# A fused attention and gated feed-forward kernel on one core: wide attention layout from the second unit, all of the first unit's weights in two parts, a new written order and three aligned places

## The chip, the core and the metric

The kernel runs on one core of a Trainium2 chip. The metric is the device time of one execution in microseconds (us). The kernel before took 614.35 us (median of three runs, 613.45 to 615.07).

## The reference

```python
# q, k, v: (8, 8, 576, 64); window 64, causal
scores = q @ k.T / 8, masked to 0 <= row - col < 64
attn = softmax(scores) @ v                 # per head
x = attn, heads side by side               # (8, 576, 512)
x_prev = x shifted by one row, zeros first # per batch
xk = mu_k * x + (1 - mu_k) * x_prev
xr = mu_r * x + (1 - mu_r) * x_prev
kk = relu(xk @ w_k) ** 2                   # (8, 576, 1024)
out = sigmoid(xr @ w_r) * (kk @ w_v)       # (8, 576, 512)
```

The three weight matrices are 64-bit floats in memory; all else is 32-bit.

## The kernel before, in words

**Units.** The 4608 rows (8 batches of 576) are cut into nine units of 512. A unit needs three products, computed transposed: r (`r_units`: 4 output tiles of 128, each summed over 4 chunks of 128 inputs), k (`k_units`: 8 tiles, 4 chunks) and v (`v_units`: 4 tiles, 8 chunks). That is 16 + 32 + 32 = 80 pieces of 128x128 by 128x512. I write R0, K0, V0 for the products of the first unit, R1, K1, V1 for those of the second.

**A product in two parts.** A piece is normally three fp32r matmuls: weight and input are each split into a high and a low part, and high*high, high*low and low*high are added up (`product`, `weight`). So a 512-column weight block must be decoded and split before it is used, and so must the mixed input. `DIRECT = "rk"` makes an exception: in the first unit, r and k use the unsplit weight (tile `whole`) and the unsplit input (tile `xm`) in one fp32 matmul per piece, which the compiler issues as two instructions. The weights are split later, for the second unit.

**Weights.** There are 20 blocks of 128x512 (`chunks`): 0 to 3 are w_r, 4 to 11 w_k, 12 to 19 w_v. For each, `decode` makes a 32-bit number out of the 64-bit one in five steps: sign (ACT), clamp (DVE or POOL), shift, top and low (DVE). Then come first_part (a cast, ACT or POOL) and second_part (a subtraction, POOL or DVE), which split it.

**Mixing.** `mix` makes xr and xk of one chunk: diff, blend (DVE), from the second unit on seam, and, where the product is split, high (cast) and low (subtraction).

**Attention.** A unit has four groups (a pair of heads each), so there are 36 groups and 18 pairs j = 0 to 17 of groups. The first unit (groups 0 to 3, `WHOLES = 4`) uses full 128x128 blocks and TensorE transposes. Later groups work in bands of 32 rows: `scores` multiplies in 64x32 tiles of the array; softmax runs on DVE and ACT (`soften`); DVE transposes; `values` multiplies in 32x64 tiles; `run_x` copies the result out. Below `WIDE = 8` a group's four bands each hold four blocks, so `values` takes 6 steps of 8 matmuls per group. From `WIDE` on a pair of groups shares bands: two bands of a group with eight blocks each, 5 steps of 8 matmuls per group, and one accumulation over both groups of the pair. In that layout the scores of a group need both groups' loads.

**The order.** The program is straight-line, and each engine works its instructions in order. The order is computed while the program is built: every piece of work has a key, costs in ns, needs and holds on buffers. `play` steps through time and lets each engine start the piece with the lowest key that is ready. For the first part of the program this choice is overruled by `ORDER`, a written list of piece numbers per engine: about 850 pieces, up to about 145 us. After that the keys decide, with a fixed pattern per unit. `clocked` models TensorE's time of a piece.

**Aligned places.** `values` can emit `addr_align`, which pads TensorE's instruction stream with empty slots until the next instruction stands at a given offset in a block of so many 64-byte slots; if more than `max_nops` slots are needed, the stream jumps over them. `PLACED = 18` makes this never happen in the kernel before, since j ends at 17.

Every operation is recorded through one helper, line 166, so the profile's rows are told apart by their tiles: `bank<-xm,whole` is an fp32 product, `bank<-xs,ws` a split r or k product, `bank<-ks,ws` a v product, `bank<-qk` scores, `bank<-pt,v` values, `ws<-` the split of a weight, `xs<-` that of an input, `ks<-` that of k squared.

## Time and profile before

| | |
|---|---|
| median of three runs | 614.35 us |
| the profiled execution | 613.81 us |
| its span on the core | 612.0 us |
| TensorE matmul busy | 596.7 us |
| DVE, ACT, POOL busy | 395.0, 371.0, 141.9 us |
| granted TensorE clock | 1.0 in every slice |

PE is TensorE's matmuls, PEld its weight loads, DVE the vector engine, ACT the scalar engine, POOL GpSimd, SP the engine that issues the loads and stores. Matmul ends are modelled, so the distance between two starts is a better length of a run of matmuls than its busy time.

### The profile page before, as it was taken

The numbers are of one execution on the slowest core, as the hardware profiler recorded it, in microseconds if no ns is written. First come the engines' busy times: TensorE is split into PE (matmuls) and PEld (weight loads), VectorE is DVE, ScalarE is ACT, GpSimd is POOL, SyncE is SP. The second block draws the span as 40 slices with busy tenths as digits, with TensorE's granted clock in tenths as the row PEclk, the third lists the DMA queues.
The fourth block names the chain that finished last, engine by engine and source line by source line (L and its number), as shares of the span: only waits on it lengthen the run. The fifth ranks groups of instructions, "written<-read, shape, count | busy, mean of one in ns | idle before, by whom it ended". The sixth has DMA issues, their size and how long they took to land.

```text
span 612.0 us, 17692 instructions
## 1 busy us (share of the span) xinstructions
PE 596.7 (98%) x7072; PEld 465.6 (76%) x7072; DVE 395.0 (65%) x1208; ACT 371.0 (61%) x1060; POOL 141.9 (23%) x208
## 2 busy tenths in 40 slices
PE   4999999999999999999999999999999999999997
PEld 3654577878888888888888888877888888888885
DVE  4899999909783667556763677276827583665211
ACT  5988967448476736683577358644766466734630
POOL 6575557502300230011201130023002300201000
PEclk9999999999999999999999999999999999999999
DMA  8997122213431223122312222132212230010001
GB/s 252 337 331 224 54 86 81 70 51 83 132 93 43 76 73 116 29 75 71 101 42 59 91 77 74 44 109 80 76 44 93 74 97 24 2 54 17 1 18 52
DMA packets 57426, 53.59 MB, mean 88 GB/s; under 512 B 10496, under 2 KB 50944, under 8 KB 57344
## 3 DMA queue, kind: packets, MB, share of 16 engines
q1 hardware_dynamic: 57344, 52.46, 28.1%
q8 instruction: 56, 0.92, 0.6%
q14 instruction: 26, 0.21, 0.1%
HBM read 43.00 MB, written 9.44 MB: 86 GB/s over the span
## 4 chain that ended last, share of the span: by engine, by line
PE 88%; DMA 7%; ACT 2%; DVE 1%; SPq 1%; issue 1%; ACTq 0%
PE bank L166 88%; DMA raw<-w_v 3%; DMA v<-v 2%; SPq L166 1%; DMA raw<-w_k 1%; DMA qk<-kT 1%; ACT pr L166 1%; DVE bank L166 1%; ACT kf L166 1%; DVE r L166 0%; ACT ws L166 0%; ACT wt L166 0%; DVE rs L166 0%; ACT ks L166 0%; DVE whole L166 0%
## 5 line engine op out<-in xcount | busy, mean ns | idle before, releaser
L166 PE MATMUL bank<-xs,ws 128*128 128x512 f32 x1152 | 273.2, 396 | 0.0
L166 PEld LDWEIGHTS bank<-xs,ws 128*128 128x128 f32 x1152 | 215.8, 188 | 50.9
L166 PE MATMUL bank<-ks,ws 128*128 128x512 f32 x864 | 206.7, 397 | 1.4 <-issue 1.4
L166 PEld LDWEIGHTS bank<-ks,ws 128*128 128x128 f32 x864 | 161.0, 188 | 40.2 <-issue 1.5
L166 DVE TENSOR_TENSOR ks<-kf,ks 128x512 fp32r<-128x512 f32 x69 | 51.1, 746 | 112.9 <-ACT ks L166 112.9
L166 ACT ACTIVATE pr<-pr,nmax 128x96 f32<-128x96 f32 (+1 forms) x288 | 105.0, 366 | 11.7 <-DVE nmax L166 11.1
L166 ACT ACTIVATE kf<-bank 128x512 f32<-128x512 f32 x72 | 43.0, 597 | 67.3 <-PE bank L166 65.4
L166 POOL CAST ks<-kf 128x512 fp32r<-128x512 f32 x8 | 4.9, 611 | 256.0 <-ACT kf L166 256.0
L166 DVE CUSTOM_DVE_ANT_0 pr<-bank,bands 128x96 f32<-128x96 f32 x256 | 49.4, 249 | 13.4 <-PE bank L166 13.2
L166 ACT COPY xT<-bank 128x256 f32<-128x256 f32 (+1 forms) x46 | 15.7, 391 | 65.1 <-PE bank L166 64.9
L166 ACT ACTIVATION_READ_ACCUMULATOR pr<-pr,nmax 128x1 f32 x288 | 54.1, 188 | 0.0
L166 ACT ACTIVATE kf<-kf 128x512 f32<-128x512 f32 x71 | 44.7, 631 | 1.9
L166 DVE SCALAR_TENSOR_TENSOR r<-bank,r 128x512 f32<-128x512 f32 x36 | 24.5, 680 | 32.3 <-PE bank L166 32.3
L166 PE MATMUL bank<-xm,whole 128*128 128x512 f32 x96 | 43.8, 601 | 1.0 <-DVE whole L166 1.0
L166 ACT ACTIVATE th<-bank 128x512 f32<-128x512 f32 x36 | 21.3, 591 | 35.8 <-PE bank L166 24.6
L166 PEld LDWEIGHTS bank<-pt,v 32*64 32x64 f32 (+1 forms) x2720 | 35.7, 131 | 9.4 <-issue 7.1
L166 ACT CAST ks<-kf 128x512 fp32r<-128x512 f32 x64 | 39.5, 619 | 1.7
L166 PE MATMUL bank<-qk 64*32 64x96 f32 (+1 forms) x2112 | 33.4, 254 | 7.3 <-DMA qk<-qT 5.9
L166 PEld LDWEIGHTS bank<-qk 64*32 64x32 f32 (+1 forms) x2112 | 28.2, 108 | 15.3 <-issue 12.5
L166 PE MATMUL bank<-pt,v 32*64 32x96 f32 (+3 forms) x2720 | 38.6, 243 | 0.3 <-ACT kf L166 0.3
L166 DVE TENSOR_TENSOR xs<-d,xs 128x512 fp32r<-128x512 f32 x59 | 37.9, 685 | 0.0
L166 ACT CAST xs<-d 128x512 fp32r<-128x512 f32 x49 | 28.8, 617 | 14.2 <-POOL d L166 12.7
(79 smaller groups left out, 547.4 us busy)
## 6 DMA issues: line engine op xcount, KB each, us to landing
v<-v SPq DMA_DIRECT2D x76, 64.0 KB, 2.1
raw<-w_k SPq DMA_DIRECT2D x8, 512.0 KB, 7.2
raw<-w_v SPq DMA_DIRECT2D x8, 512.0 KB, 5.6
v<-v SPq DMA_DIRECT2D x52, 48.0 KB, 2.0
v<-v SPq DMA_DIRECT2D x68, 32.0 KB, 2.0
raw<-w_r SPq DMA_DIRECT2D x4, 512.0 KB, 6.0
outT<-r SPq DMA_DIRECT2D x8, 256.0 KB, 2.1
qk<-kT SPq DMA_DIRECT2D x8, 224.0 KB, 4.2
```

The source lines that it names most:

```text
L166: return lambda *args, **kw: tc.keep_in_program_order(op(*args, **kw))
```

## The change

`DIRECT` becomes empty, so the first unit's r and k are split products like all others: three fp32r matmuls instead of two fp32 instructions per piece, and `mix` does high and low for the first unit too. `WIDE` becomes 4, so pairs 2 and 3 (the second unit) get the layout with two bands and eight blocks, and their loads are made in pairs of groups. The mask that was made for the third unit is made once for both layouts' first blocks. `play` charges TensorE for a change between tiled (attention) and untiled matmuls (`ENTER`, `LEAVE`), some costs are new, and `ORDER` is a new list. `values` aligns TensorE's stream ahead of pairs 3, 6 and 11.

In the new list TensorE does `S4` between the two transposes of group 2, then R0; scores 8 and 9 stand together (apart before), values 4 and 5 and values 8 and 9 too, and scores 10 and 11 come before most of K1.

```diff
-DIRECT = "rk"
+DIRECT = ""
-WIDE = 8
+WIDE = 4
-ALIGN, SKIP = 102, 12
-PLACED = 18
+PLACES, SKIP = {3: 228, 6: 59, 11: 59}, 12
+ENTER, LEAVE = 95, 281
 ORDER = {
...
-        moved, clock = 0, [WINDOW, 0, True]
+        moved, clock, tiled = 0, [WINDOW, 0, True], None
...
-                        free[e] = p.done = clocked(now, p.costs[e])
+                        work, at = p.costs[e], now
+                        before, tiled = tiled, work not in (440, 697, WHOLE)
+                        if before is not None and tiled != before:
+                            at = clocked(at, ENTER if tiled else LEAVE, 1)
+                        free[e] = p.done = clocked(at, work, 1.8 if tiled else 2.37 if work == 440 else 1.92)
...
-            if j >= PLACED:
-                tc.keep_in_program_order(nc.tensor.addr_align(128, offset=ALIGN, max_nops=SKIP))
+            if j in PLACES:
+                tc.keep_in_program_order(nc.tensor.addr_align(256, offset=PLACES[j], max_nops=SKIP))
...
-        if g >= NC:
-            load_qk(g, key=begin(g - 1) - 1)
-            load_v(g, key=begin(g) - 1)
+        for x in range(g, g + 2) if g >= WIDE and g % 2 == 0 else [g] if NC <= g < WIDE else []:
+            load_qk(x, key=begin(x - 1) - 1)
+            load_v(x, key=begin(x) - 1)
...
-            built = chain["masks"] = Piece("POOL", begin(g) - 4, 900, lambda e: first_mask(e, 0), [built, chain["least"]], port=True)
+            built = chain["masks"] = Piece("POOL", begin(g) - 4, 900, lambda e: first_mask(e, 0, 2), [built, chain["least"]], port=True)
...
-        if 2 * j % NC == 0 and u in (2, 4):
+        if 2 * j % NC == 0 and u == 4:
```

## Rows read from the trace of the kernel before

**Rows 1.** The page's first part: busy us, share, instructions of each engine.
```profile
PE 596.7 (98%) x7072; PEld 465.6 (76%) x7072; DVE 395.0 (65%) x1208; ACT 371.0 (61%) x1060; POOL 141.9 (23%) x208
```

**Rows 2.** Windows: stretch, length, busy of PE, PEld, DVE, ACT, POOL, clock, DMA.
```profile
15.00:30.00 15.00, 15.00 (x238) 10.06 (x232) 13.29 (x61) 13.66 (x52) 8.58 (x15) 1.00 0.94 332
30.00:45.00 15.00, 15.00 (x153) 8.17 (x148) 14.24 (x39) 13.49 (x38) 11.59 (x15) 1.00 1.02 336
45.00:60.00 15.00, 14.04 (x95) 5.99 (x94) 14.93 (x31) 14.35 (x33) 7.22 (x8) 1.00 0.77 236
60.00:78.00 18.00, 17.65 (x270) 9.14 (x272) 17.25 (x61) 15.64 (x51) 10.67 (x18) 1.00 0.23 63
78.00:98.00 20.00, 20.00 (x429) 15.97 (x415) 19.69 (x34) 13.04 (x26) 10.04 (x11) 1.00 0.20 58
98.00:118.00 20.00, 20.00 (x88) 16.16 (x87) 19.60 (x56) 12.81 (x48) 16.00 (x15) 1.00 0.39 115
...
123.00:166.50 43.50, 43.50 (x608) 35.22 (x608) 24.71 (x72) 25.40 (x70) 10.17 (x15) 1.00 0.32 90
```

**Rows 3.** Timeline of PE, later part: start, length, operation, count, idle before.
```profile
156.22 2.06 PE L166 MATMUL bank<-pt,v 32*64 32x96 f32 x160
158.21 8.63 PE L166 MATMUL bank<-ks,ws 128*128 128x512 f32 x36
...
204.29 1.73 PE L166 MATMUL bank<-qk 64*32 64x96 f32 x128
205.95 14.27 PE L166 MATMUL bank<-ks,ws 128*128 128x512 f32 x60
...
415.82 8.65 PE L166 MATMUL bank<-ks,ws 128*128 128x512 f32 x36 [1.36 <-issue]
...
552.50 33.63 PE L166 MATMUL bank<-xs,ws 128*128 128x512 f32 x144
585.97 22.45 PE L166 MATMUL bank<-ks,ws 128*128 128x512 f32 x96
```

**Rows 4.** Timeline of PE, one unbroken run of fp32 products.
```profile
35.33 10.57 PE L166 MATMUL bank<-xm,whole 128*128 128x512 f32 x24
```

**Rows 5.** Timeline of PE, 71 to 125 us.
```profile
73.86 1.65 PE L166 MATMUL bank<-ks,ws 128*128 128x512 f32 x6
75.36 1.88 PE L166 MATMUL bank<-xm,whole 128*128 128x512 f32 x4
77.16 1.31 PE L166 MATMUL bank<-pt,v 32*64 32x96 f32 x96
78.40 7.93 PE L166 MATMUL bank<-ks,ws 128*128 128x512 f32 x33
86.26 2.40 PE L166 MATMUL bank<-pt,v 32*64 32x96 f32 x192
88.59 5.14 PE L166 MATMUL bank<-ks,ws 128*128 128x512 f32 x21
93.67 1.00 PE L166 MATMUL bank<-qk 64*32 64x96 f32 x64
94.60 1.66 PE L166 MATMUL bank<-ks,ws 128*128 128x512 f32 x6
...
123.11 1.17 PE L166 MATMUL bank<-pt,v 32*64 32x96 f32 x80
124.21 0.96 PE L166 MATMUL bank<-xs,ws 128*128 128x512 f32 x3
```

**Rows 6.** Groups by form: busy us, mean ns of one, idle before.
```profile
L166 ACT ACTIVATE pr<-pr,nmax 128x96 f32<-128x96 f32 x256 | 92.6, 363 | 7.6 <-DVE nmax L166 7.1
...
L166 ACT CAST xs<-d 128x512 fp32r<-128x512 f32 x49 | 28.8, 617 | 14.2 <-POOL d L166 12.7 <-DVE d L166 0.8 <-PE bank L166 0.6
```

**Rows 7.** Timeline of DVE: second parts of blocks 13 and 19, the last mix.
```profile
72.01 0.69 DVE L166 TENSOR_TENSOR ws<-wt,ws 128x512 fp32r<-128x512 f32 x1
72.61 0.25 DVE L166 CUSTOM_DVE_ANT_0 pr<-bank,bands 128x96 f32<-128x96 f32 x1
...
96.94 0.69 DVE L166 TENSOR_TENSOR ws<-wt,ws 128x512 fp32r<-128x512 f32 x1
97.54 0.25 DVE L166 CUSTOM_DVE_ANT_0 pr<-bank,bands 128x96 f32<-128x96 f32 x1
...
116.95 0.68 DVE L166 TENSOR_TENSOR xs<-d,xs 128x512 fp32r<-128x512 f32 x1
117.55 0.42 DVE L166 TENSOR_SCALAR r<-r 128x512 f32<-128x512 f32 x1
```

**Rows 8.** Timeline of DVE at 88 us, one subtraction.
```profile
88.09 1.77 DVE L166 TENSOR_TENSOR ws<-whole,ws 128x512 fp32r<-128x512 f32 x1
```

**Rows 9.** Timeline of POOL at 87 us, one subtraction.
```profile
87.58 1.74 POOL L166 TENSOR_TENSOR ws<-whole,ws 128x512 fp32r<-128x512 f32 x1
```

**Rows 10.** Timeline of DVE, the first shift of a weight block.
```profile
8.60 0.69 DVE L166 TENSOR_SCALAR bank<-wt 128x512 uint32<-128x512 uint32 x1 [0.87 <-POOL wt L166]
```

**Rows 11.** The page's third part: queue, packets, MB, share of 16 engines.
```profile
q8 instruction: 56, 0.92, 0.6%
```

## The prediction

> **What bounds the kernel now.** I read the page's busy times first: PE is busy for 596.7 of the 612.0 us span [rows 1], so the end is PE's work plus 15.3 us in which it idles. Then I read the windows, to see where another engine is full as well [rows 2]. There are two stages. Up to about 118 us PE and DVE are both full (45 to 60 us: PE 14.04 and DVE 14.93 of 15; 78 to 118 us: PE 40.00 and DVE 39.29 of 40), and ACT nearly so up to 60 us (13.66 and 14.35 of 15). From 123 us on PE alone is full: DVE has 24.71 us of work in 43.5. So work taken from PE after 118 us shortens the program one for one. Work taken before it does so only if DVE, ACT and POOL deliver their products as much sooner. The timeline of PE gives the length of each run of matmuls [rows 3 to 5], that of DVE the moments when weight blocks are ready [rows 7].

> **What PE loses.** (a) R0 and K0 are 48 pieces of two fp32 instructions. A run of 24 of them takes 10.57 us [rows 4], 0.44 us each, so all 96 take 42.3 us. The new products are 48 x 3 = 144 fp32r matmuls, and a run of exactly 144 stands in the trace: from 552.50 to 585.97, 33.5 us [rows 3]. That is -8.8 us. (b) Pairs 2 and 3 in the wide layout: half of pair 2 takes 78.40 - 77.16 = 1.24 us, two halves 2.48, pair 3 at one go 88.59 - 86.26 = 2.33 [rows 5]; a wide pair takes 158.21 - 156.22 = 1.99 [rows 3]. That is -0.5 and -0.3. (c) Joined groups: scores of one group take 94.60 - 93.67 = 0.93 [rows 5], of two together 205.95 - 204.29 = 1.66 [rows 3]: -0.2 for groups 8 and 9. Values 8 and 9 apart take 1.10 each [rows 5], together 1.99: -0.2. With every join PE also changes between tiled and untiled matmuls once less; I estimate 0.1 each for three joins, since a wide pair of two halves differs from one go by no more than 0.2: -0.3. (d) The only unexplained stop of PE after 123 us, 1.36 us at 415.82, ended by nothing that the profile shows ("issue") [rows 3]. The sum is -11.7 us: the span would be 600.3 if PE idled no more than before.

> **The stop of 1.36 us.** The queue that carries instructions moved 56 packets and 0.92 MB [rows 11]. That is 16.4 KB each, and TensorE's 14,144 matmuls and weight loads [rows 1] over 56 are 253, so a packet looks like a block of 256 instructions. In the steady pattern one pair is followed by the next after about 822 TensorE instructions (half a unit: 240 matmuls with 240 loads, 128 scores and 160 values with as many, and some waits), which is 54 or 55 more than three blocks. So each pair's values stand 54.5 slots further in a block, and a position comes back after five pairs. One pair in thirteen stopped, so the bad positions are few. Aligning pairs 6 and 11 at slot 59 fixes slots 59, 113, 168, 222 and 21 for nearly all later pairs. If none is bad, 1.36 us go; if one is, two or three pairs stop and 1.4 to 2.7 us are added. I take the first, as twelve of thirteen pairs pass. The jump over the padding is not in the trace of before: at least nothing, at most one such stop at each of three places, 4.1 us. I take nothing, because PE's rows just ahead of values are long untiled runs that give the fetch time, and keep 4.1 for the range.

> The row shows one stop and no jump. [...]

> **What the other engines gain.** The first unit's mixing needs 8 casts and 8 subtractions more. The splits of the k and r weights, made up to 114 us so far, are now needed before R0 and K0 run. I counted DVE's written lists up to the second part of block 13, without which the third v piece cannot run: 144 operations before, 154 after. There are 6 more second parts (7 against 1), 6 more low parts of mixing and 2 fewer subtractions for k squared; the rest nets -0.4 us. One such subtraction takes 72.61 - 72.01 = 0.60 us [rows 7], so 10 x 0.60 - 0.4 = 5.6 us. Before, this second part ended at 72.61, so now 78.2. One credit: DVE idled 0.87 us ahead of its first shift, because POOL did the clamp late [rows 10]; in the new list DVE clamps block 0 itself and shifts it ahead of the first softmax. That makes 77.3.

> PE must get there too. The last K0 pieces need the second part of block 11, which stands 5.3 us of DVE operations ahead of block 13's: 72.0. Then PE has four K0 pieces, values 4 and 5 and two V0 pieces: 4 x 0.70 + 2.0 + 2 x 0.70 = 6.2, so the third V0 piece starts at about 78.3.

> What is left for PE at that moment: before, from 75.36 (the last four fp32 instructions) it was 612.0 - 75.36 = 536.6. Off come these four (1.8) and values 5 (1.2) [rows 5], which are done by then now, and 0.3 for pair 3, 0.4 and 0.3 for joins and 1.4 for the stop: 531.2. So unbroken, the span is 78.3 + 531.2 = 609.5.

> From there on DVE must keep up. Between the second parts of blocks 13 and 19 DVE's new list holds 22.1 us of operations at undisturbed lengths (start to start where nothing stops DVE, as the 0.60 above for one on 128x512), and PE's 26 pieces, scores 8 and 9 and values 6 and 7 take 26 x 0.70 + 1.66 + 1.99 + 0.2 = 22.1: level. Before, DVE needed 97.54 - 72.61 = 24.9 us [rows 7] for 21.6 us of operations, so 3.3 were lost, mostly beside POOL: a subtraction of 0.60 took 1.77 while POOL did one in 1.74 [rows 8, 9]. POOL's new list holds about 18 us of work for the stage where it held 26.0 (78 to 118 us) [rows 2], so I put the loss at 0 to 2.3, middle 1.2. DVE is 1.0 ahead of PE at the start, so 0.2 reaches PE: 609.7. The bounds are 609.5 and, with the whole 3.3, 611.8.

> The loads: values of groups 4 to 7 bring five blocks per band instead of six, at no cost. Scores of group 4 now wait for group 5's loads too, with a transpose and R0 queued behind; some 1.5 us at most at 26 us, where PE will wait for split weights anyway. POOL makes one mask less. I take nothing for these.

> The profiled execution took 613.81 us, 1.8 over its span, so 609.7 becomes **611.5 us**. The median of before stands 0.5 above that execution; I leave this in the range.

> **Rivals.**
> *The decoders become the bound (slower).* PE has pieces for K1 only when the last mixed chunk of the second unit is split, on DVE. The place is that subtraction. Behind block 13 DVE's list holds 38.7 us up to it. Before, DVE took 117.55 - 72.61 = 44.9 us [rows 7] for 36.3 us of operations there, 1.24 times as long; with this factor it is 77.3 + 48.0 = 125.3, 491.3 us of PE's work are left, and the time is 618.4. It decides from 120.7 us on; each us later is a us. For it: DVE was full to 118 us, and ACT, which idled 9.3 us from 60 to 98 us [rows 2], gets 10 us more up to the cast of block 19 (ten exps of 0.36 and eight casts of 0.62 [rows 6], and three diffs). Against it: some of the 1.24 was DVE waiting for PE, and POOL does less. Likely size 614 to 618.4.
> *PE never waits longer (all of it).* 600.3 + 1.8 = 602.1. For it: ACT and POOL idled 20 and 39 us from 15 to 118 us [rows 2]. Against: DVE's count above.
> *The aligned places stop PE.* 611.5 + 1.4 (the stop stays) to + 4.1 (three jumps): 612.9 to 615.6. [...]

> **Chances.** Forecast 0.56, decoders 0.22, aligned places 0.14, all of it 0.08. A measurement of this kernel can tell about 0.3%, 1.8 us, from no change: below 612.5 is faster, above 616.2 slower. The forecast, which spreads by some 2 us, gives 0.43 faster and 0.13 same. The decoders give 0.05 same and 0.17 slower. The places give 0.04 faster, 0.08 same, 0.02 slower. The last is faster. In all 0.55, 0.26, 0.19. The range of 605.5 to 617.5 leaves out the full gain and the far end of the decoders' case.

> **What would show it.** Right: no fp32 rows (`xm,whole`); some 10 us more idle of PE, before 78 us, ended by DVE or ACT at ws or xs; the second part of block 13 on DVE at 77 to 79 us; from there PE without gaps; no stop of over 1 us ended by "issue"; wide pairs 2 and 3 of 2.0 us. Wrong: gaps of PE after 80 us that end with DVE's xs or ws (decoders), stops ended by "issue" at pairs 3, 6, 11 or every fifth pair (places), or no idle in the first stage (all of it).

## The result, and the profile after

The changed kernel takes 620.12 us (median of six runs, 619.01 to 621.52) against 614.75 for the one before: ratio 1.0098, 95% interval 1.0082 to 1.0115. I had forecast 611.5. It is 1% slower, and the forecast was wrong in size and in sign. The profiled execution took 619.93 us with a span of 617.8, and its mean granted clock is 0.988.

The busy times, the answer to [rows 1]: PE works less, as forecast, and the span is longer all the same.

```profile
PE 593.7 (96%) x7056; PEld 477.7 (77%) x7056; DVE 395.1 (64%) x1217; ACT 379.6 (61%) x1076; POOL 129.8 (21%) x195
```

What PE waited for (releaser: us in total, times, longest). The waits on DVE, ACT and POOL are short ones before 73 us. The line to look at is "issue", time in which nothing that the profile shows held PE: 5.7 us in four stops, where before had one of 1.4.

```profile
PE bank L169 <- DMA qk<-qT: 6.1, 2, 5.2
PE bank L169 <- issue: 5.7, 4, 1.9
PE bank L169 <- DVE xs L169: 2.7, 4, 1.4
PE bank L169 <- ACT pt L169: 1.9, 2, 1.7
```

Where they are, from PE's timeline (start, length, operation, count, idle before). Each splits a values group:

```profile
72.84 2.89 PE L169 MATMUL bank<-pt,v 32*64 32x96 f32 x159
77.23 0.24 PE L169 MATMUL bank<-pt,v 32*64 32x32 f32 x1 [1.50 <-issue]
77.40 7.24 PE L169 MATMUL bank<-ks,ws 128*128 128x512 f32 x30
...
94.10 1.92 PE L169 MATMUL bank<-pt,v 32*64 32x96 f32 x141
96.77 0.47 PE L169 MATMUL bank<-pt,v 32*64 32x96 f32 x19 [0.75 <-issue]
...
284.28 1.95 PE L169 MATMUL bank<-pt,v 32*64 32x96 f32 x144
288.13 0.35 PE L169 MATMUL bank<-pt,v 32*64 32x32 f32 x16 [1.90 <-issue]
288.41 10.18 PE L169 MATMUL bank<-ks,ws 128*128 128x512 f32 x36
...
354.16 8.63 PE L169 MATMUL bank<-ks,ws 128*128 128x512 f32 x36
...
448.43 1.94 PE L169 MATMUL bank<-pt,v 32*64 32x96 f32 x143
451.94 0.35 PE L169 MATMUL bank<-pt,v 32*64 32x96 f32 x17 [1.57 <-issue]
452.22 15.76 PE L169 MATMUL bank<-xs,ws 128*128 128x512 f32 x60
```

The stops are at pairs 2, 3, 9 and 14. Pairs 9 and 14 are five apart, the distance after which a position in a block of 256 instructions comes back. And the 36 `ks,ws` matmuls behind the stop at pair 9 take 10.18 us where 36 take 8.63 elsewhere; the 60 `xs,ws` behind pair 14 take 15.76 where 60 in this trace take 14.21 (at 115.06). The windows say why (the clock stands after the five busy times):

```profile
286.00:288.00 2.00, 0.23 (x17) 0.04 (x3) 0.00 (x0) 0.00 (x0) 0.00 (x0) 1.00 0.13 37
288.00:290.00 2.00, 1.87 (x20) 1.52 (x21) 1.42 (x4) 1.23 (x3) 0.00 (x0) 0.68 0.35 91
290.00:292.00 2.00, 2.00 (x6) 1.56 (x5) 1.35 (x2) 1.62 (x4) 1.21 (x3) 0.50 0.14 32
292.00:294.00 2.00, 2.00 (x9) 1.60 (x9) 0.94 (x2) 1.61 (x3) 0.26 (x1) 0.97 0.19 53
294.00:296.00 2.00, 2.00 (x10) 1.62 (x9) 2.00 (x4) 0.48 (x2) 1.45 (x2) 1.00 0.44 145
```

PE stood still, and behind it the granted clock is 0.50 for some 3 us: 10.18 - 8.63 = 1.55 us more. Pair 14 is the same: 1.55. So the two late stops cost 3.45 and 3.1 us, twice what the profile calls a wait.

Two other places matter for the argument. DVE's subtraction for block 13, and its last of the second unit's mixing:

```profile
74.98 0.68 DVE L169 TENSOR_TENSOR ws<-wt,ws 128x512 fp32r<-128x512 f32 x1
...
118.71 0.69 DVE L169 TENSOR_TENSOR xs<-d,xs 128x512 fp32r<-128x512 f32 x1
```

### The profile page after: what moved, and what is told of

It reads as the page before. It is cut to its first block, busy times and chain, and to the rows that moved or that the text cites. A ratio compares the mean times of both kernels' runs of the same rounds, so it can differ in the third digit from the quotient of the medians.

```text
span 617.8 us, 17666 instructions
## 1 busy us (share of the span) xinstructions
PE 593.7 (96%) x7056; PEld 477.7 (77%) x7056; DVE 395.1 (64%) x1217; ACT 379.6 (61%) x1076; POOL 129.8 (21%) x195
## 4 chain that ended last, share of the span: by engine, by line
PE 90%; DVE 4%; DMA 3%; issue 1%; SPq 1%; ACT 1%; DVEq 0%
PE bank L169 90%; DMA qk<-kT 1%; DMA raw<-w_r 1%; DVE bank L169 1%; DVE pr L169 1%; DVE ws L169 1%; DMA v<-v 1%; DVE wt L169 1%; SPq L169 1%; DVE d L169 0%; DVE xs L169 0%; ACT d L169 0%; ACT pr L169 0%; DVE rs L169 0%; DVE r L169 0%
## 5 line engine op out<-in xcount | busy, mean ns | idle before, releaser
L169 PE MATMUL bank<-xs,ws 128*128 128x512 f32 x1296 | 312.1, 399 | 3.3 <-DVE xs L169 2.7
L169 PEld LDWEIGHTS bank<-xs,ws 128*128 128x128 f32 x1296 | 244.4, 190 | 63.1 <-DVE xs L169 4.3
L169 DVE TENSOR_TENSOR ks<-kf,ks 128x512 fp32r<-128x512 f32 x67 | 48.5, 725 | 96.1 <-ACT ks L169 94.1
L169 PEld LDWEIGHTS bank<-pt,v 32*64 32x64 f32 (+1 forms) x2656 | 35.2, 130 | 15.3 <-issue 11.7
L169 DVE TENSOR_TENSOR xs<-d,xs 128x512 fp32r<-128x512 f32 x64 | 42.5, 700 | 0.9 <-POOL xs L169 0.8
L169 ACT CAST xs<-d 128x512 fp32r<-128x512 f32 x56 | 33.2, 618 | 14.4 <-POOL d L169 12.7
L169 DVE COPY xT<-bank 128x256 f32<-128x256 f32 x21 | 8.3, 422 | 45.4 <-PE bank L169 45.4
```

The source lines that it names most:

```text
L169: return lambda *args, **kw: tc.keep_in_program_order(op(*args, **kw))
```

## The experiments

A *slot* is an instruction's position in a block of 256 of TensorE's stream, counted in the built program from an aligned place. A values group has 321 instructions. In the stretch ahead of any aligned place I count back from the stop itself. In the kernel before, the stop came right behind the 160th matmul of pair 13, so a border lay 320 instructions behind the group's start, at slot 512 - 320 = 192.

The theory formed from the four stops: at slots 192, 229, 223 and 224 the group stopped after 159, 141, 144 and 143 matmuls, that is after 318, 282, 288 and 286 instructions, each within two of the second border (512 less the slot: 320, 283, 289 and 288). A group that crosses two borders uses up a whole block in 1.6 us (160 matmuls in 1.99), and, so the theory, the block behind it is not there yet.

**1. Other places** (`a_moved`).

```diff
-PLACES, SKIP = {3: 228, 6: 59, 11: 59}, 12
+PLACES, SKIP = {2: 40, 3: 40, 6: 74, 11: 74}, 12
```

> The changed kernel with other aligned places: pairs 2 and 3 at slot 40 of a block of 256, pairs 6 and 11 at slot 74 (59 before), so that the values of pairs 2 to 17 start at 41, 41, 111, 137, 75, 129, 184, 238, 37, 75, 130, 184, 239, 37, 90, 144. Theory 1 (slots): a values group of 321 slots stops TensorE when it starts between about 190 and 230 of a block, as the four stops did (192, 229, 223, 224). Here none does: no stop ended by issue, no low clock after 30 us, span 617.8 - 1.50 - 0.75 - 1.90 - 1.57 - 1.56 - 1.55 = 609.0 us, time about 611. If the stop at pair 2 only covered a wait for the split weights, 610.5. Rival (first stage): the loss is the idle time and the low clock before 30 us, which PE never makes up; the span stays at 615 or more. Rival (jumps): stops come from the jumps over the padding; there are four jumps now, so at least as many stops.

614.69 us, ratio to before 0.9998 (0.9985 to 1.0010). Most of the loss is gone, but not all stops are: 0.95 and 0.77 us stay at pairs 8 and 13, slot 184, where the border lies 328 instructions on, just behind the group, and 0.66 us at pair 3, behind a jump. Pairs 9 and 14 (238, 239) pass.

**2. The places alone, in the kernel before** (`b_places`).

```diff
-ALIGN, SKIP = 102, 12
-PLACED = 18
+PLACES, SKIP = {6: 59, 11: 59}, 12
...
-            if j >= PLACED:
-                tc.keep_in_program_order(nc.tensor.addr_align(128, offset=ALIGN, max_nops=SKIP))
+            if j in PLACES:
+                tc.keep_in_program_order(nc.tensor.addr_align(256, offset=PLACES[j], max_nops=SKIP))
```

> The kernel before with only the aligned places of pairs 6 and 11 at slot 59. Its values then start at 225 (pair 9), 224 (pair 14) and 169 (pair 13, 192 before). Theory 1 (slots): stops at pairs 9 and 14 of 1.4 to 1.9 us, each followed by a stretch at the lower clock that costs about as much again, none at pair 13: span 612.0 - 1.4 + 2 x 3.3 = 617.2, time about 619, nearly all of the loss of the changed kernel, from the places alone. Rival (first stage, or loads of the new layout): the places are harmless in the old order; span 610.6, time 612.4.

617.18 us, 1.0047 (1.0032 to 1.0062): two numbers make the old kernel slower, with nothing else changed. The profiled execution is the quickest of seven (613.89) and has one stop, at pair 14, without a lower clock behind it; pair 9 (slot 225) passed there. The six others took 615.73 to 618.15 us, 1.8 to 4.3 more; that pair 9 stops in them, or that the clock falls behind pair 14, could account for it, but was not seen.

```profile
443.75 1.94 PE L165 MATMUL bank<-pt,v 32*64 32x96 f32 x143
447.60 0.35 PE L165 MATMUL bank<-pt,v 32*64 32x96 f32 x17 [1.92 <-issue]
447.88 12.35 PE L165 MATMUL bank<-xs,ws 128*128 128x512 f32 x52
```

**3. No places** (`a_none`): `PLACES = {}`.

> The changed kernel without any aligned place. The values of pairs 2 to 17 then start at 192, 134, 204, 230, 25, 79, 134, 188, 243, 41, 96, 150, 205, 3, 56, 110. Theory 1 (slots): stops at pairs 2, 4 and 14 (192, 204, 205), none or short ones at 188 and 230; two or three of them followed by a lower clock: span 617.8 - 0.75 - 3.5 - 3.1 + 2 x 3.3 = 617 (615 where one keeps the clock). Rival (jumps): no jump, no stop: span 610. Rival (first stage): 615 or more with no stop.

620.38 us, 1.0094 (1.0075 to 1.0112). Stops at 192 (1.74), 204 (1.48), 188 (1.12) and 205 (1.60, with the low clock: the 60 `xs,ws` behind it take 15.76). So the places neither gained nor lost against none: without them as many stops are there. The rival (jumps) falls, since there is no jump here.

**4. A survey of slots** (`a_survey`): `PLACES = {2: 40, 3: 40, 4: 178, 6: 134, 8: 146, 10: 158, 12: 172, 14: 180, 16: 184}`.

> The changed kernel with a place ahead of pairs 2, 3 (slot 40), 4, 6, 8, 10, 12, 14 and 16, so that the pairs reached without a jump start at 205 (pair 5), 189 (7), 201 (9), 213 (11), 227 (13), 235 (15), 239 (17) and those behind a jump at 41, 41, 179, 135, 147, 159, 173, 181, 185. One run that reads off which slots stop TensorE. Theory 1 (slots): stops at 201, 205, 213 and 227, none at 235 and 239 and none behind a jump; 189 is the edge. The stop grows shorter the later in the group the second block's border comes (201: border 311 slots in; 227: 285 slots in). Rival (jumps): stops behind the jumps, or at all of them.

One run, 625.17 us, eight stops. Two of them, from its timeline, are at slots 205 and 201; only the second is followed by the low clock (10.18 for 36):

```profile
156.42 1.99 PE L169 MATMUL bank<-pt,v 32*64 32x96 f32 x153
160.44 0.31 PE L169 MATMUL bank<-pt,v 32*64 32x32 f32 x7 [2.03 <-issue]
160.69 8.63 PE L169 MATMUL bank<-ks,ws 128*128 128x512 f32 x36
...
287.89 2.01 PE L169 MATMUL bank<-pt,v 32*64 32x96 f32 x155
291.55 0.31 PE L169 MATMUL bank<-pt,v 32*64 32x32 f32 x5 [1.64 <-issue]
291.78 10.18 PE L169 MATMUL bank<-ks,ws 128*128 128x512 f32 x36
```

All profiles of this study together, for pairs reached in sequence (225 was seen in one execution; pair 3 stands apart, see 6 and the open points):

| slot | stop, us |
|---|---|
| 169 to 176 | none |
| 184, 188, 189 | 0.77 to 0.95, 1.12, 1.11 |
| 192, 201, 204, 205 | 1.36 to 1.74, 1.64, 1.48, 1.60 and 2.03 |
| 213, 223, 224 | 1.82, 1.90, 1.57 and 1.92 |
| 225, 227 to 230, 235 to 247 | none |

My expectation missed 227, which passes, and a stop's length doesn't shrink toward 224. Behind a jump, 179, 181 and 185 stopped for 0.24 to 0.88.

The theory of two borders doesn't give the upper edge, since a group at 225 to 247 crosses two as well. The trace's records of the single instruction packets show the difference. At 184 to 224 the packet starts 1.0 to 2.1 us into the group; at 225 to 247 it starts 1.5 to 3.1 us ahead of it (`b_places`: 1.14 us into the group at 224, 1.52 ahead at 225). And in all 27 stops of these profiles, pair 3's too, PE goes on 1.2 to 1.6 us after a packet has ended. So I take it that PE stops for the next block of instructions; what makes its packet start so much earlier one slot on is not shown.

**5. One number** (`a_64`).

```diff
-PLACES, SKIP = {3: 228, 6: 59, 11: 59}, 12
+PLACES, SKIP = {3: 228, 6: 64, 11: 64}, 12
```

> The changed kernel with one number changed: pairs 6 and 11 at slot 64 instead of 59, pair 3 as it was. Pairs 9 and 14 then start at 228 and 229 instead of 223 and 224. Theory 1 (slots): the stops of 1.90 and 1.57 us and the two stretches of low clock behind them (1.56, 1.55 us) are gone, those at pairs 2 and 3 stay: span 617.8 - 6.6 = 611.2 us, time 613.5 us. Rival (first stage and its low clock before 30 us): 617 or more.

613.95 us, 1.0001 (0.9988 to 1.0013). By the ratio, five slots give back the whole loss. The stops at pairs 2 and 3 stay (1.55 and 0.74 us); pairs 9 and 14 pass without a gap, and the clock stays at 1.00 there:

```profile
285.08 2.06 PE L169 MATMUL bank<-pt,v 32*64 32x96 f32 x160
287.08 8.17 PE L169 MATMUL bank<-ks,ws 128*128 128x512 f32 x34
...
445.56 2.06 PE L169 MATMUL bank<-pt,v 32*64 32x96 f32 x160
```

**6. All stops away** (`a_good`, `a_best`, `a_best2`). Three tries at pairs 2 and 3, with 64 for pairs 6 and 11.

```diff
-PLACES, SKIP = {3: 228, 6: 59, 11: 59}, 12
+PLACES, SKIP = {2: 40, 6: 64, 11: 64}, 12            # a_good
+PLACES, SKIP = {6: 64, 11: 64}, 12                   # a_best
+EARLY = {6: 115}
...
+        if g in EARLY:                                # in scores(g)
+            tc.keep_in_program_order(nc.tensor.addr_align(256, offset=EARLY[g], max_nops=SKIP))
...
+PLACES, SKIP = {2: 164, 4: 40, 6: 64, 11: 64}, 12    # a_best2
```

> The changed kernel with places at pair 2 (slot 40), 6 and 11 (slot 64), so that pairs 2 to 17 start at 41, 239, 53, 79, 65, 119, 174, 228, 27, 65, 120, 174, 229, 27, 80, 134: all outside 178 to 227, where the stops of the earlier runs began, and pair 3 reached without a jump. Theory 1 (slots; the price of the places is the whole difference between forecast and result): no stop ended by issue after 60 us; span 612.2 - 0.66 - 0.95 - 0.77 = 609.8 us, where the first such version stood at 612.2, and the time about 612.2, 0.4% under before. Rival (decoders): what the stop at pair 3 gives back is taken by waits for weights behind it, and the span stays at 610.5 or more.

> The changed kernel with the early place ahead of the scores of group 6 instead of values: the jump then lies 23 us before pair 3, and pairs 2 to 5 start at 66, 8, 78, 104; pairs 6 and 11 at slot 64. Theory 1 (slots, and a jump shortly before a group or a late fetch at pair 3 as the cause of its stop of 0.99 us): no stop after 60 us at all; 613.2 - 1.0 = 612.2 us. Rival (decoders): waits for weights take the place of the stop, 613.0.

> The changed kernel with places at pair 2 (slot 164), 4 (slot 40), 6 and 11 (slot 64): pairs 2 to 17 start at 165, 107, 41, 67, 65, 119, 174, 228, 27, 65, 120, 174, 229, 27, 80, 134. Pair 3 now starts in the middle of a block and without a jump; in the version without places it did so at 134 and did not stop. Theory 1 (slots, at pair 3 with a fetch that starts late): no stop after 60 us, span 610.2 us, time 612.2. Rival: pair 3 or the jumps stop TensorE again, 613.0.

613.21 (0.9975; 0.9961 to 0.9988), 612.85 (0.9979; 0.9966 to 0.9991) and 611.25 us (0.9961; 0.9947 to 0.9974). The first two still stop at pair 3, at slot 239 for 0.99 us and at slot 8 for 0.53, here at its first border. In the third pair 3 starts at 107, no stop is left, and the time is what I had forecast for the change. What PE waits for in it; the "issue" line is gone:

```profile
PE bank L169 <- DMA qk<-qT: 6.2, 2, 5.4
PE bank L169 <- DVE xs L169: 2.4, 4, 1.4
PE bank L169 <- ACT pt L169: 1.8, 1, 1.8
...
PE bank L169 <- DVE wt L169: 0.7, 2, 0.4
PE bank L169 <- DVE ws L169: 0.5, 1, 0.5
```

**7. The old kernel without its stop** (`b_good`): the edit of 2 with 64 for 59.

> The kernel before with only two aligned places, pairs 6 and 11 at slot 64: the values of pair 13 start at 174 instead of 192, all others outside 178 to 227. Theory 1 (slots): the one stop of 1.36 us is gone, with the low clock that some executions have behind it: span 610.6 us, time 612.5 to 613.2. Rival: stops hit other pairs instead, no gain (614.6).

612.75 us, 0.9962 (0.9947 to 0.9977), as much as `a_best2`. So with the stops taken out on both sides, no gain from all else in the change can be told from nothing. The two ratios leave room for some 1.2 us either way. The profiled spans, 610.0 here and 609.1 in `a_best2`, differ by 0.9 us, and no more than that stood in my forecast besides the stop (612.0 to 609.7 is 2.3, of which 1.4 is the stop).

**8. Parts alone** (`w_only`, `a_rk`). Both have `DIRECT = "rk"` and 64 for pairs 6 and 11; `w_only` has the list of the kernel before, `a_rk` the new list, less the 16 pieces that are then not made.

> One part alone: the wide layout from the second unit on, with the first unit's weights unsplit again for its r and k products (fp32 matmuls), the list of the kernel before, and places at slot 64 for pairs 6 and 11. Theory 1: 0.8 us less of PE's work in pairs 2 and 3 and no stop: span 609.8, time 611.8 to 612.4, so that the layout gives what was forecast. Rival (loads): the old list brings the loads of groups 5 and 7 too late for the scores of 4 and 6, which now need both; a wait of 1 to 3 us at 26 or 54 us, time 613 to 615.

> The changed kernel (its list, its layout, places at slot 64 for pairs 6 and 11) with the first unit's r and k products as unsplit fp32 matmuls again, and without the 16 casts and subtractions of its inputs. Theory 2 (the 8.8 us that PE saves in R0 and K0 are given back as its waits for the splits, 14 us idle before 73 us): PE now works 8.8 us longer there but waits less; time within 1.5 us of the version with split products. Rival (the saving is real): 6 to 8 us slower than that version, 618 or more.

`w_only`: 623.06 us, 1.0123 (1.0098 to 1.0147), worse than its rival said. Its timeline shows the wait that I had priced at nothing for the new list, since scores of group 4 now need both groups' loads (and the `v` loads are late too). The run of four fp32 instructions behind it takes 2.71 us, 1.98 in `b_good`:

```profile
30.10 1.49 PE L169 MATMUL bank<-qk 64*32 64x96 f32 x52 [2.62 <-DMA qk<-qT]
31.52 2.71 PE L169 MATMUL bank<-xm,whole 128*128 128x512 f32 x4
...
79.65 0.98 PE L169 MATMUL bank<-pt,v 32*64 32x96 f32 x60 [1.41 <-DMA v<-v]
```

It also stops at pair 3 (slot 240) for 1.44 us. So with the old list the new layout loses 8 us, and not all of that is the list's.

`a_rk`: 614.26 us, 0.9983 (0.9970 to 0.9995). With 8.8 us more of PE work, by the forecast's count, it is by the ratios 0.22% (some 1.4 us) behind `a_best2`; the profiled spans, 612.4 and 609.1, differ by 3.3. PE reaches pair 2 at 76.50 in it, hardly idle from 28 us on, and at 73.22 in `a_best2`, also 3.3 apart. So between 1.4 and 3.3 of the 8.8 us are kept, and my expectation (within 1.5) and its rival (6 to 8) both miss the upper figure.

**9. Is DVE what PE waits for there?** (`a_pool`, `a_twice`). `a_pool` is `a_best` with two subtractions moved from DVE to POOL. `a_twice` is `a_best2` with six of them done twice:

```diff
-            engines[e].tensor_sub(x2[0][:, 1], state[0], x2[0][:, 0].bitcast(F32))
+            for _ in range(2 if u == 0 and e == "DVE" else 1):
+                engines[e].tensor_sub(x2[0][:, 1], state[0], x2[0][:, 0].bitcast(F32))
```

> As the last one, and the subtractions of the first unit's k inputs of chunks 1 and 2 (0.69 us each on DVE at 48.9 and 52.1 us) moved to POOL, right behind their casts there, where POOL idled. Theory 2 (DVE's list sets when the split weights are ready up to 75 us, so PE's saving in R0 and K0 is given back): block 13's second part comes 1.3 us sooner and the time falls by 0.6 to 1.3 us, to about 611.2. Rival (POOL slows DVE as much as it relieves it, or ACT is the gate): no change, 612.2, or slower.

> The last version with one cost doubled: each of the six subtractions of the first unit's inputs that DVE does is done twice (0.69 us each, 4.1 us in all before block 13's second part). Theory 2 (DVE's list sets when PE may go on up to 75 us): block 13's second part comes 4 us later and the time grows by 3 to 4 us, to 615.5 to 616. Rival (ACT, the loads or PE itself are the gate): under 1 us.

`a_pool` didn't do what I wanted: 613.10 us, 0.9985 (0.9973 to 0.9996), no gain. The second parts of blocks 11 and 13 started at 70.03 and 76.52 on DVE instead of 69.16 and 75.66, and PE followed by the same 0.86 (the piece that waits for `ws` at 71.85, not 70.99). The two subtractions took 1.62 and 1.35 us on POOL, and beside them three of DVE's operations took 1.6 us more (0.68, 0.41 and 1.10 us in `a_best`; 1.18, 0.87 and 1.78 here), against 1.36 taken off DVE. That is the rival. The stop at pair 3 is longer too in the profiled execution, 1.08 us against 0.53.

`a_twice`: 616.14 us, 1.0034 (1.0022 to 1.0046). Block 13 moves from 75.36 to 79.74, pair 2 on PE from 73.22 to 77.61, by 4.4 us both, and the time grows by 4.9. So DVE's list is the gate up to pair 2, microsecond for microsecond.

```profile
79.74 0.69 DVE L169 TENSOR_TENSOR ws<-wt,ws 128x512 fp32r<-128x512 f32 x1
```

```profile
75.08 2.60 PE L169 MATMUL bank<-xs,ws 128*128 128x512 f32 x10 [0.53 <-DVE ws L169]
77.61 2.90 PE L169 MATMUL bank<-pt,v 32*64 32x96 f32 x160
```

**The low clock before 30 us** needed no run of its own. In the changed kernel the clock is 0.50 from 24 to 28 us, behind short waits of PE (1.74 and 1.28 us). `a_moved` has it too, `a_good` hasn't. `a_moved`:

```profile
24.00:26.00 2.00, 2.00 (x68) 1.67 (x67) 2.00 (x7) 2.00 (x7) 0.68 (x5) 0.50 0.96 378
26.00:28.00 2.00, 2.00 (x27) 1.58 (x8) 1.97 (x10) 2.00 (x7) 0.68 (x1) 0.50 1.03 403
```

`a_good`:

```profile
24.00:26.00 2.00, 1.24 (x59) 1.07 (x66) 2.00 (x9) 1.37 (x5) 1.61 (x7) 1.00 0.90 274
26.00:28.00 2.00, 1.98 (x39) 1.38 (x23) 1.97 (x5) 2.00 (x8) 0.00 (x0) 1.00 0.99 334
```

DVE is full in both, and the piece that waits for `ws` starts at 70.89 and 70.99. Here, where DVE is the gate, the slow clock cost PE nothing.

## Why the prediction was wrong, point by point

**The step that failed: the aligned places.** The part "The stop of 1.36 us" said of slots 59, 113, 168, 222 and 21: "I take the first, as twelve of thirteen pairs pass." The reading of the stream was right (blocks of 256, steps of 54.5, five pairs a cycle); measured starts are 60, 114, 169, 223 and 22. For half a unit it writes 240 matmuls with 240 loads; it is 120 with 120 (60, 36 and 24 between two pairs), and with these the sum comes near the 822 that it uses. The choice was wrong. One stop in thirteen says little of five places spread evenly round the circle: the stopping slots reach from about 180 to 224, 45 wide, and four of the five gaps between neighbours are 54.5 wide (the fifth 38), so only 4 x 9.5 of 256 phases miss them, one in seven. 64 passes because 174 and 228 lie just outside on either side. The trace of before held more than I took from it. Its stop lay behind the 160th matmul, so that pair started at 192, and counting on in steps of 822.5 its pairs at 176, 230 and 247 passed. 223 lies in the gap between the known bad slot and the next known good one, which I should have called an even chance. In the runs pairs 9 and 14 stopped there (223 and 224), and 64 in place of 59 took both stops away (`a_64`).

**The price of a stop** was the second error of the same step. I took 1.36 us from the one row [rows 3], with full speed behind it. Here two of the four were followed by 1.55 us lost at a granted clock of 0.50. The rival with the places ended at 615.6. It named the right cost, but its ground, the jumps, was not the cause: `a_none` stops as often without any. It had too few stops and half the price for the late ones, and 0.14 was too little.

**The sum, with the stops put in.** From the third V0 piece I forecast 531.2 us to the end. After: that piece starts six matmuls into the run at 77.40, at 78.8, and 617.8 - 78.8 = 539.0. The difference of 7.8 is 0.75 + 1.90 + 1.57 in stops, 1.55 + 1.55 in low clock (7.3 together), and 0.5 in small ones. In `a_best2` the piece starts at 77.5 to 77.7, and 609.1 less that is 531.5. The forecast span of 609.7 is met at 609.1. For the start of that piece this is in part luck: DVE was earlier and pair 2 longer than I had counted (both below), and the two partly cancel.

**DVE's count.** Block 13's second part ended at 75.66; forecast 77.3. Block 11's ended at 70.25 (68.48 + 1.77, beside POOL); forecast 72.0. Both came 1.7 us sooner than I counted; the stop of 1.50 us at pair 2 used up what this gave.

**(a) R0 and K0.** No `xm,whole` row is left, and the `xs,ws` products went from 273.2 us of busy time to 312.1, 38.9 for 144 matmuls instead of 33.5, with the low clock in it (35.9 in `a_best2`). The saving on PE is real and most of it was given back, as the count of DVE said: PE idled 8.4 us from 15 to 78 us (sum of the windows) against 1.3 [rows 2], 1.5 of it in the stop. That is 7 more where I expected some 10; the low clock at 24 to 28 us fills most of the rest.

**(b), (c).** Pair 3 takes 1.99 us where it isn't stopped (`a_best2`, 93.69 to 95.68), scores 8 and 9 together 86.23 - 84.57 = 1.66, values 8 and 9 together 131.19 - 129.20 = 1.99, all as forecast. Pair 2 takes 2.9, not 2.0: its first matmuls come in gaps of 0.1 to 0.3 us. In `a_best2` a wait of 0.24 us of their weight loads ends with ACT reading a k product out of its bank (`kf`), and one of 0.17 with nothing that the profile shows; the rest is open.

**(d)** The stop at pair 13 is gone, as forecast; it moved to pair 14.

**The decoders** didn't become the bound: the subtraction that decides ended at 119.40, before 120.7, with no gap of PE around it. But by the forecast's own span it decides from 609.7 - 491.3 = 118.4 on; 120.7 goes with the 612.0 of before. In `a_best2` it ended at 117.89, so the rival was nearer than its place in the prediction says.

**Loads.** Nothing, as taken; but `w_only` shows that this is the list's doing.

**The jumps** cost nothing at pairs 6 and 11, as taken. The 4.1 us that the rival set against three of them, three stops of 1.36, were my estimate. Here no stop falls on a jump itself (each goes less than one block ahead), and borders in unbroken sequence cost up to 2.03 us.

Open: why pair 3 stops at slots 229, 239, 240 and 8, where later pairs at 229 and 239 pass. In `a_good` the instruction queue's packet starts 0.46 us after pair 3 begins (slot 239, 94.43 us) and 1.85 us before pair 9 does (slot 228, 282.51). There PE had waited 0.41 us for DVE shortly before pair 3; but in `w_only` (slot 240) it had run without a gap from 79.65 us up to the stop, its packet was as late (0.56 us), and the stop was longer. So that wait of PE is not what it takes. Open too is what decides whether the clock falls behind a stop: by the lengths of the matmuls behind, it did at 1.57, 1.60, 1.64, 1.82 and 1.90 us, not at 1.36, 1.48, 1.50, 1.55, 1.74, 1.92 and 2.03.

## What to carry to other kernels

Where short tiled matmuls run in long groups, count where each group starts in TensorE's blocks of 256 instructions, and take from every stop and every pass in the trace which starts are bad; one stop with its place known tells more than a rate of one in thirteen. Price a stop of TensorE with the matmuls behind it (1.55 us more behind two of the four here), not by its idle time alone. And compare a change with the old kernel at its own best places: here the moved borders cost 1%, and the rest of the change was worth no more than the noise hides, some 1.2 us.
